# Attention into a gated MLP on one core: PSUM score banks lent to four steps of the second h phase, and small VectorE work moved around it

## The chip, the cores and the metric

The kernel runs on one core of one Trainium2 chip. The metric is the device time of one execution in microseconds; for each kernel the median of several runs is taken. One further execution is taken with the hardware profiler, and all durations of single instructions come from that one.

## The reference, cut to what matters

Eight batches, eight heads, 512 local tokens and 32 global tokens of width 64. Local queries see the global keys and a window of 32 keys on either side; global queries see all keys. The 544 tokens of each batch then go through an MLP with a gate of the quick-gelu form.

```python
s_g = scale * q_g @ concat(k_g, k_l).T         # global queries: all keys
out_g = softmax(s_g) @ concat(v_g, v_l)
s_ll = where(abs(i - j) <= 32, scale * q_l @ k_l.T, -1e9)
s_lg = scale * q_l @ k_g.T                     # local queries: global keys + window
out_l = softmax(concat(s_lg, s_ll)) @ concat(v_g, v_l)
x = concat(out_g, out_l) as (tokens, heads * 64)         # 512 features
h = x @ w_in                                   # 512 -> 2048
out = (h * sigmoid(1.702 * h)) @ w_out         # 2048 -> 512
```

Inputs and outputs are float32; the products run on bf16 operands with float32 sums.

## The kernel before, in words

**Units of work.** A batch's eight heads are two groups of four; a group is one object, `a` (heads 0 to 3) and `c` (heads 4 to 7) of the batch in hand. Batches 0 and 1 use the class `Quad`, batches 2 to 7 the class `Wide`. The objects of batch 2 are `nq[2]`.

**What an object does.** `Tk` turns k (VectorE stream transpose of a 128x512 tile, line 525, and a copy of a part of it, line 527), `Tq` turns q (line 308), `ext` places the group's global queries around the turned q and the global keys into the turned k (four small VectorE copies, lines 536 to 540, from `qgT` and `kgT`, which `transpose_g` fills, line 238). `S(0)` and `S(1)` are the two rounds of scores: TensorE writes them into a *pair* (`spair`): two PSUM tiles of two banks each, named s0 and s1. `X` is the exponential, one ScalarE instruction for each of the two tiles (line 562), `M` the multiplication with the mask on VectorE (line 567). `U(0)` to `U(2)` sum weights and values on TensorE, `Gm` does so for global queries, and `R`, `XL` and `G` divide and store the result as the MLP's input (`xL`, `xG`) on VectorE. For batch 2 onward `UG` is `U` and `Gm`, `RXG` the divisions.

**The MLP.** For a batch i, `h_step(i, fc)` runs one of 16 steps: four matmuls of 512 columns into one PSUM bank (`h_mm`, line 606), tanh of it on ScalarE into `th` (line 613), and on VectorE the product of 1 + tanh and the bank (line 614), which is the gate's output `gT`. `th` has two buffers. The banks come from `pbank`, a pool of four one-bank tiles, which also serves the sums of `U`, `Gm` and the output. `phase_o(i)` then multiplies with `w_out` in four blocks of 16 matmuls (`o`, line 631), and each block is evicted on ScalarE (line 645) and stored.

**Order.** The program is written out by hand: `manual_schedule` keeps each engine's queue in the order in which the Python code issues instructions. Each engine runs its queue in order; semaphores between the engines are placed by the framework, from which instruction touches which tile. The attention of batch i + 1 stands between the h phase and the four o blocks of batch i: at the end of an h phase, `a.S(0)` of the next batch has been done; `phase_o` begins with `c.T()`, `c.ext()`, `a.S(1)`, `a.X(1)`, `a.M(1)`, `o(0)`, `c.S(0)`, `a.UG()`.

**The second h phase** (i = 1) is written out apart from the others, since it still has work of batch 2 in it. Its four first half-steps and the extra work per step read:

```python
for fc, kcs in ((0, (0, 1)), (1, (0, 1)), (0, (2, 3)), (1, (2, 3))):
    h_mm(1, fc, hps[fc], kcs)
for fc in range(FC):
    h_act(1, fc, hps[fc]) if fc < 2 else h_step(1, fc)
    if fc == 1: nq[1][1].G()
    if fc == 2: a.Tk()
    if fc == 7: transpose_g(4, 6, "q"); a.ext()
    if fc == 10: a.S(0); a.X(0)
a.M(0)
```

Just before it, the same pair of score tiles holds sums of batch 1: `a.Gm` in bank 0 and the three sums of `c` in banks 1 to 3; `c.XL` and `a.G` read them last. `nq[2][0].Tq()` and `transpose_g(4, 6, "k")` stand behind `a.R()` of batch 1.

## Time and profile before

| | |
|---|---|
| median of 3 runs | 303.69 us (303.2 to 304.45) |
| the profiled execution, as timed | 303.15 us |
| its span, first to last instruction | 301.4 us |
| TensorE busy | 292.7 us, 97% |
| VectorE busy | 218.3 us, 72% |
| ScalarE busy | 167.3 us, 56% |
| GpSimd busy | 75.5 us, 25% |
| share of the chain that ended last | TensorE 84%, VectorE 5%, DMA 4%, ScalarE 4% |
| mean granted TensorE clock | 1.000 |

In the profile's lines PE is TensorE, PEld its weight loads, DVE VectorE, ACT ScalarE, POOL GpSimd and SP the queue that issues output DMAs. A line of a timeline gives start (us from the start of the span), duration (us; of a merged group, first start to last end), engine, source line, operation, tiles and shape, count, and in brackets the engine's idle time before it and what ended it. In the list of groups by form, the two numbers behind the bar are the total in us and the mean of one in ns. Matmuls overlap: each shows some 0.38 us of 512 columns, and one starts every 0.216 us.

The stage at issue, by the trace's windows: from 54.07 to 69.74 us (second h phase) TensorE is busy 15.14 of 15.67 us, VectorE 12.91 and ScalarE 10.77; from 90.50 to 104.31 us (third h phase) TensorE is busy 13.81 of 13.81 us, VectorE 10.20 and ScalarE 9.55.

### The profile page before, as it was taken

Reading aid. Unit: us, or ns where it says so; the run is one execution under the profiler, and the core shown is the slowest. Engines: PE = TensorE matmul, PEld = TensorE weight load, DVE = VectorE, ACT = ScalarE, POOL = GpSimd, SP = SyncE. Lnnn points to the kernel's source line nnn. Section 1 sums busy time; section 2 is a strip of 40 time slices with the busy share of each in tenths; the row PEclk is TensorE's granted clock in tenths of the full one; section 3 lists DMA queues with packets and bytes.
Section 4 is the critical chain, followed back from the end, with each engine's and each line's share of the span. In section 5 each row is a group of like instructions: output and inputs, shape, how many; then the busy total and the mean of one; then the engine's idle time right before and its main releaser. Section 6 shows DMA issues by size and latency. Waiting matters only on the chain.

```text
span 301.4 us, 8146 instructions
## 1 busy us (share of the span) xinstructions
PE 292.7 (97%) x3409; PEld 150.1 (50%) x3409; DVE 218.3 (72%) x445; ACT 167.3 (56%) x258; POOL 75.5 (25%) x126
## 2 busy tenths in 40 slices
PE   6899999998999999999999999999999999999995
PEld 6454445443554455445454455445454455446653
DVE  6578857879976887778967887788877866683320
ACT  4838484476537756476446736567447651763421
POOL 8742655972045000900054002600000000000000
PEclk9999999999999999999999999999999999999999
DMA  7999999999459512990269412900220012101122
GB/s 191 178 209 209 206 180 226 123 181 183 66 78 145 100 37 54 124 153 7 70 70 145 86 38 72 124 0 11 63 63 10 0 48 64 35 0 28 44 69 71
DMA packets 59220, 28.35 MB, mean 94 GB/s; under 512 B 47664, under 2 KB 49072, under 8 KB 59184
## 3 DMA queue, kind: packets, MB, share of 16 engines
q0 software_dynamic: 51024, 17.57, 51.9%
q1 hardware_dynamic: 7680, 9.61, 12.0%
q10 hardware_dynamic: 480, 0.66, 0.7%
q8 instruction: 26, 0.43, 0.6%
q14 instruction: 10, 0.08, 0.1%
HBM read 36.31 MB, written 8.91 MB: 150 GB/s over the span
## 4 chain that ended last, share of the span: by engine, by line
PE 84%; DVE 5%; DMA 4%; ACT 4%; issue 1%; SPq 0%; ACTq 0%
PE op L631 35%; PE hp L606 33%; PE ov L577 5%; PE s L551 4%; DVE gT L614 2%; DMA ek<-ek 2%; DMA g32k<-in_k_g_dram 2%; ACT th L613 1%; PE s L606 1%; ACT e L380 1%; PE ov L459 1%; PE op L643 1%; ACT e L562 1%; DVE e L567 1%; DVE kT L525 1%
## 5 line engine op out<-in xcount | busy, mean ns | idle before, releaser
L631 PE MATMUL op<-w_out_sb,gT 128*128 128x512 bf16 x528 | 121.8, 380 | 0.0
L614 DVE SCALAR_TENSOR_TENSOR gT<-th,hp 128x512 bf16<-128x512 f32 (+1 forms) x140 | 91.2, 657 | 41.3 <-ACT th L613 40.2
L606 PE MATMUL hp<-xL,w_in_sb 128*128 128x512 bf16 x496 | 109.2, 379 | 0.5 <-DVE xL L492 0.2
L613 ACT ACTIVATE th<-hp 128x512 f32<-128x512 f32 (+1 forms) x140 | 79.8, 573 | 43.9 <-PE hp L606 39.7
L606 PEld LDWEIGHTS <-w_in_sb 128*128 128x128 bf16 x576 | 56.1, 98 | 65.4 <-issue 1.8
L631 PEld LDWEIGHTS <-gT 128*128 128x128 bf16 x528 | 49.3, 98 | 55.3 <-issue 0.9
L645 ACT ACTIVATE ob<-op 128x512 f32<-128x512 f32 (+2 forms) x35 | 20.5, 585 | 71.8 <-PE op L631 69.3
L97 POOL DMA_DIRECT2D v<-in_v_l_dram x30 | 23.9, 800 | 98.3 <-PE og L588 94.0
L562 ACT ACTIVATE e<-s 128x1016 bf16<-128x1016 f32 (+1 forms) x48 | 45.7, 1005 | 1.2 <-PE s L551 1.0
L567 DVE TENSOR_TENSOR e<-e,mask 128x1760 bf16<-128x1760 bf16 (+1 forms) x24 | 25.0, 1040 | 2.2 <-ACT e L562 2.2
L483 DVE STREAM_TRANSPOSE sT<-ov 128x512 f32<-128x512 f32 x15 | 10.8, 717 | 15.5 <-PE ov L577 11.6
L492 DVE TENSOR_TENSOR xL<-ov,rs 128x512 bf16<-128x512 f32 x30 | 19.3, 686 | 1.5 <-PE ov L459 0.2
L551 PE MATMUL s<-q,kT 32*128 32x160 bf16 (+3 forms) x576 | 16.1, 243 | 0.9 <-DVE kT L540 0.9
L551 PEld LDWEIGHTS <-kT 32*128 32x128 bf16 x576 | 11.1, 94 | 11.3 <-issue 5.1
L380 ACT ACTIVATE e<-s 128x856 bf16<-128x856 f32 x14 | 11.7, 881 | 5.1 <-PE s L347 5.1
L99 POOL DMA_DIRECT2D v<-in_v_g_dram x24 | 13.9, 580 | 2.4 <-DMA rk<-in_k_l_dram 2.1
L525 DVE STREAM_TRANSPOSE kT<-rk 128x512 f32<-128x512 f32 x12 | 12.5, 1041 | 0.0
L487 DVE STREAM_TRANSPOSE rs<-rT 128x512 f32<-128x512 f32 x16 | 11.4, 711 | 0.6
L308 DVE STREAM_TRANSPOSE q<-rq 128x512 f32<-128x512 f32 (+1 forms) x17 | 11.3, 662 | 0.2 <-ACT rq L669 0.2
L577 PE MATMUL ov<-e,v 128*32 128x128 bf16 (+3 forms) x576 | 11.0, 223 | 0.0
L606 PE MATMUL hp<-xG,w_in_sb 128*128 128x256 bf16 x64 | 9.6, 273 | 0.0
L577 PEld LDWEIGHTS <-v 128*32 128x32 bf16 x576 | 9.1, 97 | 0.1
(105 smaller groups left out, 173.8 us busy)
## 6 DMA issues: line engine op xcount, KB each, us to landing
out_dram<-ob SPq DMA_DIRECT2D x132, 64.0 KB, 1.9
rk<-in_k_l_dram POOLq DMA_DIRECT2D x6, 512.0 KB, 9.4
rq<-in_q_l_dram POOLq DMA_DIRECT2D x5, 512.0 KB, 7.5
v<-in_v_l_dram POOLq DMA_DIRECT2D x24, 96.0 KB, 4.5
w_out_sb<-in_moe_w_out_dram POOLq DMA_DIRECT2D x4, 512.0 KB, 10.5
v<-in_v_l_dram POOLq DMA_DIRECT2D x14, 128.0 KB, 6.7
rq<-in_q_l_dram POOLq DMA_DIRECT2D x5, 256.0 KB, 8.9
w_in_sb<-in_moe_w_in_dram POOLq DMA_DIRECT2D x4, 256.0 KB, 6.7
```

The lines of the kernel that those rows point to most:

```text
L97: nc.gpsimd.dma_start(out=vt[0:n, :, c, :D], in_=vs[FIRST[c] : FIRST[c] + n])
L492: nc.vector.tensor_mul(self.x[:, 2 * self.u + h, :], self.st[1 + h], self.st["rs"])
L525: nc.vector.transpose(flat[:, 0:Sl].rearrange("p (r t) -> p t r", t=16), loaded[self.b][0][:, self.u].bitcast(F32))
L551: nc.tensor.matmul(bank(self.ps, j)[:, at : at + n], lhsT=self.k[p, KEYS[c] : KEYS[c] + 128, e], rhs=self.q[p, lo:hi, r0 : r0 + nr, e], st ...
L562: nc.scalar.activation(self.E[rnd][:, 2 * i : 2 * i + 2, :n], self.ps[i][:, :, :n], AF.Exp, scale=scale)
L567: nc.vector.tensor_mul(e, e, mask[:, rnd : rnd + 1, :n].to_broadcast([128, 4, n]))
L577: nc.tensor.matmul(ov[32 * j : 32 * j + 32, :].rearrange("p (t r) -> p t r", t=16)[:, t0:t1, r0 : r0 + nr], lhsT=lv, rhs=self.E[rnd][:, j, ...
L606: nc.tensor.matmul(hp[:, : width(i)], lhsT=w_in_c[:, fc // 8, kc, fc % 8 // 2, :, fc % 2], rhs=(xL[i] if i < B else xG)[:, kc, :], start=( ...
L613: nc.scalar.activation(th[:, :n], hp[:, :n], AF.Tanh, scale=0.851)
L614: nc.vector.scalar_tensor_tensor(gTs[i][:, fc, :n], in0=th[:, :n], scalar=1.0, in1=hp[:, :n], op0=ALU.add, op1=ALU.mult)
L631: nc.tensor.matmul(op, lhsT=gTs[i][:, fc, tci * 128 : tci * 128 + 128], rhs=w_out_sb[:, fc, :], start=(first and fc == 4 * f4), stop=(fc = ...
L645: nc.scalar.activation(ob[:, lo:hi], op[:, lo:hi], AF.Copy, scale=0.5)
```

## The change

Five edits, all but the last in or just before the second h phase:

1. `nq[2][0].Tq()` and the transpose of batch 2's global k move from behind `a.R()` to behind `c.M(0)` of batch 1.
2. `a.Tk()` of batch 2 moves from behind step 2 to the front of the phase, the transpose of global q from step 7 to step 1, and `nq[1][1].G()` from step 1 to step 2.
3. Steps 2 to 5 take the four banks of a new pair of score tiles (banks 2, 3, 0, 1, so steps 2 and 3 share tile s1, steps 4 and 5 tile s0) in place of banks of the pool.
4. The four copies of `a.ext()` go to ScalarE, one behind the tanh of each of steps 3 to 6, and three of the four of `c.ext()` behind those of steps 7 to 9; the fourth stays on VectorE. The two exponentials of `a.X(0)` stand behind the tanh of step 10 and of step 11.
5. `ext` addresses the same bytes as two-byte elements, twice as many, in all phases, so also where its copies stay on VectorE.

```diff
-        def ext(self):
+        def ext(self, parts=range(4), copy=None):
+            copy = copy or nc.vector.tensor_copy
+            qt = self.qt.bitcast(BF16)
+            qg = qgT[:, self.Q, :].bitcast(BF16)
             def g(n, r, m):
-                src = qgT[:, self.Q, : n * r].rearrange("p (t o r) -> p t o r", o=1, r=r)
-                return src.to_broadcast([128, n, m, r])
-            ends = self.qt[:, 0:4, :].rearrange("p t (g r) -> p t g r", r=8)
-            nc.vector.tensor_copy(ends[:, :, 0:4:3], g(4, 8, 2))
-            nc.vector.tensor_copy(self.qt[:, 20:23, 4:28].rearrange(...), g(3, 12, 2))
-            nc.vector.tensor_copy(self.qt[:, 1:4, 10:22], qgT[:, self.Q, :36].rearrange(...))
-            nc.vector.tensor_copy(self.kT[:, :, 96:128], kgT[:, self.Q : self.Q + 1].to_broadcast([128, 4, 32]))
+                src = qg[:, : 2 * n * r].rearrange("p (t o r) -> p t o r", o=1, r=2 * r)
+                return src.to_broadcast([128, n, m, 2 * r])
+            if 0 in parts:
+                copy(qt[:, 0:4, :].rearrange(...)[:, :, 0:4:3], g(4, 8, 2))
+            if 1 in parts:
+                copy(qt[:, 20:23, 8:56].rearrange(...), g(3, 12, 2))
+            if 2 in parts:
+                copy(qt[:, 1:4, 20:44], qg[:, :72].rearrange(...))
+            if 3 in parts:
+                copy(self.kT.bitcast(BF16)[:, :, 192:256],
+                     kgT[:, self.Q : self.Q + 1].bitcast(BF16).to_broadcast([128, 4, 64]))
...
-        def X(self, rnd):
+        def X(self, rnd, halves=(0, 1)):
...
     c.M(0)
+    nq[2][0].Tq()
+    transpose_g(4, 6, "k")
     osteps(0, (2, 2), (2, 3))
...
     a.R()
-    nq[2][0].Tq()
-    transpose_g(4, 6, "k")
     c.M(1)
...
+    a.Tk()
     gTs[1] = moe.tile([128, FC, TB], BF16, name="gT")
     hps = [pbank("hp") for _ in range(2)]
     for fc, kcs in ((0, (0, 1)), (1, (0, 1)), (0, (2, 3)), (1, (2, 3))):
         h_mm(1, fc, hps[fc], kcs)
+    pt = spair()
+    hps += [bank(pt, j) for j in (2, 3, 0, 1)]
+    def on_act(out_, in_):
+        nc.scalar.activation(out_, in_, AF.Copy)
     for fc in range(FC):
         if fc < 2:
             h_act(1, fc, hps[fc])
         else:
-            h_step(1, fc)
+            h_step(1, fc, hps[fc] if fc < 6 else None)
         if fc == 1:
+            transpose_g(4, 6, "q")
+        if fc == 2:
             nq[1][1].G()
-        if fc == 2:
-            a.Tk()
-        if fc == 7:
-            transpose_g(4, 6, "q")
-            a.ext()
+        if 3 <= fc <= 6:
+            a.ext((fc - 3,), on_act)
+        if 7 <= fc <= 9:
+            c.ext((fc - 7,), on_act)
         if fc == 10:
             a.S(0)
-            a.X(0)
+            a.X(0, (0,))
+        if fc == 11:
+            a.X(0, (1,))
     a.M(0)
...
         c.T()
-        c.ext()
+        c.ext((3,) if i == 1 else range(4))
```

More of the change, by code (lines that the diff above doesn't have):

```diff
@@ L528, in Tk @@
             self.k = flat.bitcast(BF16).rearrange("p (m e) -> p m e", e=2)
-        def ext(self):
+        def ext(self, parts=range(4), copy=None):
+            copy = copy or nc.vector.tensor_copy
+            qt = self.qt.bitcast(BF16)
+            qg = qgT[:, self.Q, :].bitcast(BF16)
             def g(n, r, m):
-                src = qgT[:, self.Q, : n * r].rearrange("p (t o r) -> p t o r", o=1, r=r)
-                return src.to_broadcast([128, n, m, r])
-            ends = self.qt[:, 0:4, :].rearrange("p t (g r) -> p t g r", r=8)
-            nc.vector.tensor_copy(ends[:, :, 0:4:3], g(4, 8, 2))
-            nc.vector.tensor_copy(self.qt[:, 20:23, 4:28].rearrange("p t (g r) -> p t g r", r=12), g(3, 12, 2))
-            nc.vector.tensor_copy(self.qt[:, 1:4, 10:22],
-                                  qgT[:, self.Q, :36].rearrange("p (t r) -> p t r", r=12))
-            nc.vector.tensor_copy(self.kT[:, :, 96:128], kgT[:, self.Q : self.Q + 1].to_broadcast([128, 4, 32]))
+                src = qg[:, : 2 * n * r].rearrange("p (t o r) -> p t o r", o=1, r=2 * r)
+                return src.to_broadcast([128, n, m, 2 * r])
+            if 0 in parts:
+                copy(qt[:, 0:4, :].rearrange("p t (g r) -> p t g r", r=16)[:, :, 0:4:3], g(4, 8, 2))
+            if 1 in parts:
+                copy(qt[:, 20:23, 8:56].rearrange("p t (g r) -> p t g r", r=24), g(3, 12, 2))
+            if 2 in parts:
+                copy(qt[:, 1:4, 20:44], qg[:, :72].rearrange("p (t r) -> p t r", r=24))
+            if 3 in parts:
+                copy(self.kT.bitcast(BF16)[:, :, 192:256],
+                     kgT[:, self.Q : self.Q + 1].bitcast(BF16).to_broadcast([128, 4, 64]))
         def S(self, rnd):
@@ L557, in S @@
             self.E[rnd] = att.tile([128, 4, EW], BF16, name="e%d" % rnd)
-        def X(self, rnd):
+        def X(self, rnd, halves=(0, 1)):
             n = (EW, EW - 12)[rnd]
-            for i in range(2):
+            for i in halves:
                 nc.scalar.activation(self.E[rnd][:, 2 * i : 2 * i + 2, :n], self.ps[i][:, :, :n], AF.Exp, scale=scale)
@@ L615, in h_act, with h_step @@
                                        in1=hp[:, :n], op0=ALU.add, op1=ALU.mult)
-    def h_step(i, fc):
+    def h_step(i, fc, hp=None):
         if fc == 0:
             gTs[i] = moe.tile([128, FC, TB], BF16, name="gT")
-        hp = pbank("hp")
+        if hp is None:
+            hp = pbank("hp")
         h_mm(i, fc, hp, range(NKC))
```

## The prediction, made before the changed kernel was run

> **What bounds the kernel now.** First the page's table of engines, for what is short.

> ```profile
> PE 292.7 (97%) x3409; PEld 150.1 (50%) x3409; DVE 218.3 (72%) x445; ACT 167.3 (56%) x258; POOL 75.5 (25%) x126
> ```

> TensorE hardly rests, so a change can save only its gaps. The granted clock is 1.000, so the clock plays no part. Second, the chain of waits in order of time (start us, us, engine and line), for where a gap lies:

> ```profile
> 52.23 1.85 PE op L631 x8
> 54.07 1.29 DVE xL L492 x2
> 55.40 0.39 PE hp L606
> 55.82 0.61 ACT th L613
> 56.45 1.28 DVE gT L614 x2
> ...
> 61.60 0.70 DVE gT L614
> 62.38 0.61 ACT th L613
> 63.01 0.69 DVE gT L614
> ...
> 70.87 0.69 DVE gT L614
> 71.56 0.98 DVE e L567
> ...
> 74.89 0.68 PE s L551 x24
> 75.57 1.51 PE ov L577 x70
> ...
> 90.50 13.81 PE hp L606 x64
> ```

> Later h phases are one piece of TensorE: 64 matmuls, 13.81 us, 0.216 each, 0.863 a step. Between start-up and the last batch, the second h phase (54.07 to 74.89) is the one stage where the chain runs through VectorE and ScalarE. A th buffer pair makes the loop: tanh k waits for product k-2, and two steps take 63.01 - 61.60 = 1.41 us. Third, TensorE's timeline there:

> ```profile
> 69.74 0.66 PE L551 MATMUL s<-q,kT 32*128 32x108 bf16 x24
> 74.89 0.68 PE L551 MATMUL s<-q,kT 32*128 32x160 bf16 x24 [0.92 <-DVE kT L540]
> ```

> From 54.07 to 69.74 are 15.67 us for 13.81 of h and 0.61 of scores: 1.25 lost. Then scores 0.60 and o 3.56 end at 73.90 and the next scores start at 74.89: 0.99 lost. The sums after them take 1.51 where later phases show 1.20: 0.31 lost. So 2.55 us is all that this place can give. Fourth, VectorE's timeline before and in it:

> ```profile
> 47.72 0.72 DVE L483 STREAM_TRANSPOSE sT<-ov 128x512 f32<-128x512 f32 x1 [1.31 <-PE ov L459]
> 49.40 0.67 DVE L308 STREAM_TRANSPOSE q<-rq 128x512 f32<-128x512 f32 x1
> 49.99 0.20 DVE L238 STREAM_TRANSPOSE kgT<-rkg 128x64 f32<-128x64 f32 x1
> ...
> 58.90 1.04 DVE L525 STREAM_TRANSPOSE kT<-rk 128x512 f32<-128x512 f32 x1
> 59.98 0.30 DVE L527 COPY kT<-kT 128x192 f32<-128x192 f32 x1
> ```

> **A walk through the phase.** I go step by step with these rows: matmul 0.216 apart, a step's sum ready 0.17 after its last slot (a matmul shows 0.38); tanh 0.60, starting 0.03 after the sum and 0.08 after product k-2; product 0.69, 0.03 after its tanh, the next one 0.60 later if nothing holds it; TensorE resumes 0.05 after a VectorE end (55.35 to 55.40). For the kernel before it gives an end of h at 69.76 (trace 69.74), of product 15 at 71.48 (71.56) and of the second mask (M(1), line 567) at 75.71 (75.79). I compare walk with walk.

> **Transposes of q and global k moved up.** They leave 49.40 to 50.12 and stand after c.M(0), which ends at 46.41; VectorE then idles 1.31 us until 47.72, and they take about 0.85. Their loads were issued at 32.70 and 33.22; the slowest such load took 10.1 and 13.8 us, so they land by 47.0 at the worst. VectorE is full from 47.72 to 55.35, so all behind moves 0.73 up: the c.XL pair ends at 54.62, and the 0.22 that TensorE waits for it goes.

> **a.Tk() moved up.** 1.30 us (58.90 to 60.20), now behind a.G() (0.68) and ahead of product 0. Its load (issued 40.50, at most 9.6) lands by 50.1. Queued behind it are all products: product 0 starts at 54.54 (the pair's successor, 1.21 after 53.33) + 0.68 + 1.30 = 56.52, not 56.45, product 1 at 57.12. tanh 2 needs product 0, so 57.21 + 0.08 = 57.29; product 2 is 57.92 to 58.61. Global q's transpose (0.2) fits between; c.G() moves behind product 2.

> **Score banks for steps 2 to 5.** With more banks TensorE would not wait for early products; I expect it to wait longer. A pair of score banks is two tiles of two banks each; steps 2 and 3 share one, steps 4 and 5 the other, and each step's product is issued before the next step's matmuls. The instruction order of the changed program lists these waits (the first matmul of steps 2, 3 and 5; the first one waits on TensorE's own count):

> ```
> L613 Matmult s4_1223<-xL_758,w_in_sb_114 128x512 [waits PE_49]
> L613 Matmult s4_1223<-xL_758,w_in_sb_114 128x512 [waits DVE_49]
> L613 Matmult s4_1222<-xL_758,w_in_sb_114 128x512 [waits DVE_49]
> ```

> The counts asked for are those of product 2 and product 4: step 3 may not write its own bank until the reader of the neighbour bank is done. TensorE is in order, so all h behind it waits. Walk: step 2 is done at 56.66, step 3 resumes after 58.61, counted from 58.83: 2.17 lost. It ends at 59.69, step 4 at 60.55; tanh 4 60.58, product 4 61.21 to 61.90; step 5 from 62.12: 1.57 lost. The ten steps from there run free, with the scores, to 62.98 + 8.63 + 0.61 = 72.22. So 3.74 is added and the 1.25 removed; steps 6 and on wait for nothing, since VectorE has caught up. [...]

> **Copies on ScalarE.** Seven of 72 to 256 two-byte elements. Nearest rows: a 32-element eviction, 0.20, and the 128x160 and 128x192 mask copies, 0.49 and 0.55, which gives 0.35 to 0.65 each on their slope. In the first h phase a tanh and such a copy took 0.87 to 0.92 a step, TensorE's pace. They fall in steps 3 to 9, where ScalarE now waits on TensorE: nothing on the path at either price (last product 73.57 both ways). Without the two waits, the dear end would cost 0.4. Splitting the exponentials moves one tanh 0.9 sooner and the next later: nothing, as X is read only by M(0).

> **The end of the stage.** Product 15 ends 1.35 after h: 73.57 (71.48). Then VectorE's queue: M(0), c.T, one copy in place of four (0.28 saved), M(1). From product 15 to the end of M(1) were 4.23, now 3.95: 77.52 against 75.71. The scores start at 73.57 + 3.03 (2.78 from 71.56 to the copies at 74.34, the copy 0.2, the wake-up 0.05) = 76.60, TensorE being ready at 72.22 + 0.60 + 3.56 = 76.38: of the 0.99 remains 0.22. Behind that, TensorE has no wait until the last batch, so the shift stays: **+1.81 us**.

> **Two-byte view in the other phases.** The four VectorE copies now count twice the elements. At 107.46 to 107.87 they take 0.41; M(1) ends at 108.91, needed about 109.2. If they doubled, some 0.1 would be lost in each of five phases: 0 to 0.5, nothing gained as the slack is unused. No row of the trace is such a copy; I take 0, since the nearest rows (166 to 216 ns for 36 to 128 wide elements) are mostly a fixed part. [...] POOL's and SP's orders are unchanged.

> **Sum.** 303.15 (the profiled execution: span 301.4 and 1.75 around) + 1.81 = 304.96. The median of the runs, 303.69, is 0.54 above that run; on it I forecast **305.5 us**.

> **Rivals.** *Faster: the two waits don't bite.* Without them the walk ends h at 68.49, product 15 at 69.84, M(1) at 73.79: -1.92, 301.8 us. It decides when both waits together cost under 1.9 us. For it: nothing in the trace shows such a wait. Against: the order lists it, and product 2 cannot be early with Tk ahead. 0.06. *Only the first wait bites* (product 4 early): 3.74 - 1.57, the stage ends 0.25 late, 303.9 us. For it: ScalarE is idle there. Against: step 4's own sum, tanh and product take 1.35 after it. 0.13. *The transposes find no gap*, the XL pair stays at 55.35: both waits move with it, +2.5, 306.2 us. Against: the landings. 0.13. *The two-byte copies cost*: +2.3, 306.0 us. 0.08. The forecast keeps 0.60.

> **Numbers.** 0.5% (1.5 us) is about what a measurement can tell from no change. The forecast is 0.3 above that bound; with a spread of half a us from row times and run medians I count 0.42 of its 0.60 as slower, 0.18 as same. Slower 0.42 + 0.13 + 0.08 = 0.63; same 0.18 + 0.13 = 0.31; faster 0.06. The range 304.2 to 306.6 leaves out the faster rival and most of the one-wait case.

> **What would show it.** Right: TensorE idle about 2.0 and 1.4 us before steps 3 and 5, released by the gT product, no other gap in h; scores after o about 1.7 late; VectorE's XL pair ending near 54.6. Wrong: one h piece without gaps from 54 on (rival one), ScalarE copies over 0.65, or later scores waiting on kT's copy by more than 0.1.

## The result, and the profile after

Over 22 runs of each, the changed kernel has a median of 307.02 us (304.9 to 311.67) and the kernel before 303.74 us: ratio 1.0096, interval 1.0073 to 1.0118 (executions over 1.5% above the fastest of their kernel are left out of the ratio). It is slower, as forecast, but by 3.3 us where 1.8 were forecast, and the time lies above the range (304.2 to 306.6).

One thing is needed to read this number. In 12 of the 22 executions the mean granted TensorE clock is 0.999 or 1.000, with a median of 305.85 us. In the other ten it is 0.982 to 0.994, and these take 307.69 to 311.67 us. For the kernel before, the clock is on record for the 64 executions that were run beside the experiments below: 55 of them are at 0.997 or above, with a median of 303.77 us. So the change costs 305.85 - 303.77 = 2.08 us where the clock stays full, and the rest of the 3.3 us comes from a clock that does not.

The profiled execution of the changed kernel has a full clock: 305.89 us, span 304.0 (before 303.15 and 301.4). First, its page's table of engines:

```profile
PE 291.1 (96%) x3368; PEld 151.2 (50%) x3409; DVE 217.8 (72%) x438; ACT 168.6 (55%) x265; POOL 75.6 (25%) x126
```

TensorE's share has sunk by a point: the span grew, the work did not. (The matmul count differs from 3409 only by records that the trace lacks.) Second, TensorE's timeline in the changed stage:

```profile
54.56 1.89 PE L613 MATMUL hp<-xL,w_in_sb 128*128 128x512 bf16 x8
56.28 1.03 PE L613 MATMUL s<-xL,w_in_sb 128*128 128x512 bf16 x4
59.34 1.89 PE L613 MATMUL s<-xL,w_in_sb 128*128 128x512 bf16 x8 [2.03 <-DVE gT L621]
62.70 1.02 PE L613 MATMUL s<-xL,w_in_sb 128*128 128x512 bf16 x4 [1.47 <-DVE gT L621]
63.56 4.48 PE L613 MATMUL hp<-xL,w_in_sb 128*128 128x512 bf16 x19
...
77.45 0.68 PE L558 MATMUL s<-q,kT 32*128 32x160 bf16 x24 [0.22 <-DVE kT L546]
```

`s` is the lent score tile. TensorE idles 2.03 us before step 3 and 1.47 us before step 5, both times until a product (gT) has ended; no other gap is left in h. In the trace of the kernel before, h starts with

```profile
53.90 1.29 PE L606 MATMUL hp<-xL,w_in_sb 128*128 128x512 bf16 x5
```

so that from the first h matmul to the batch 1 scores after o the stage takes 77.45 - 54.56 = 22.89 us, against 74.89 - 53.90 = 20.99 before: +1.90. The span grew by 2.6; the other 0.7 is there ahead of the stage (h starts at 54.56 where 53.90 is before's, though nothing before 46 us was changed): ScalarE's casts in the start-up wait 2.6 us for loads of q, 0.9 in the trace of before. Two more full-clock traces of the same kernel start h at 54.26 and 54.81. Third, the chain of waits there:

```profile
57.28 1.19 DVE gT L621 x2
58.48 0.15 DVE qgT L238
58.63 0.67 DVE gT L621
...
59.34 1.90 PE s L613 x8
...
61.33 0.61 ACT th L620
...
61.96 0.70 DVE gT L621
...
62.70 1.02 PE s L613 x4
```

It goes product 0, 1, the transpose of global q, product 2, then step 3's matmuls, step 4's, its tanh, its product, step 5's matmuls: the chain of the prediction's walk. Fourth, VectorE's timeline ahead of the stage:

```profile
47.08 0.70 DVE L308 STREAM_TRANSPOSE q<-rq 128x512 f32<-128x512 f32 x1
47.71 0.20 DVE L238 STREAM_TRANSPOSE kgT<-rkg 128x64 f32<-128x64 f32 x1
...
54.02 1.29 DVE L492 TENSOR_TENSOR xL<-s,rs 128x512 bf16<-128x512 f32 x2
```

The two transposes found the gap behind the mask at line 387, and the XL pair ends at 55.31, 0.75 after h started.

### The profile page after: what moved, and what is told of

It reads as the page before. It is cut to its first block, busy times and chain, and to the rows that moved or that the text cites. A ratio compares the mean times of both kernels' runs of the same rounds, so it can differ in the third digit from the quotient of the medians.

```text
span 304.0 us, 8105 instructions
## 1 busy us (share of the span) xinstructions
PE 291.1 (96%) x3368; PEld 151.2 (50%) x3409; DVE 217.8 (72%) x438; ACT 168.6 (55%) x265; POOL 75.6 (25%) x126
## 4 chain that ended last, share of the span: by engine, by line
PE 84%; DVE 6%; DMA 4%; ACT 3%; issue 2%; SPq 0%; ACTq 0%; DVEq 0%
PE hp L613 35%; PE op L639 33%; PE ov L584 5%; PE s L558 5%; DMA ek<-ek 2%; PE s L613 2%; DMA q<-in_q_l_dram 2%; DVE gT L621 2%; ACT e L380 1%; PE ov L459 1%; DVE xL L492 1%; PE s L347 1%; PE ov L433 1%; PE op L651 1%; DVE e L574 1%
## 5 line engine op out<-in xcount | busy, mean ns | idle before, releaser
L639 PE MATMUL op<-w_out_sb,gT 128*128 128x512 bf16 x497 | 119.1, 379 | 1.9 <-issue 0.5
L621 DVE SCALAR_TENSOR_TENSOR gT<-th,hp 128x512 bf16<-128x512 f32 (+1 forms) x136 | 88.7, 655 | 41.4 <-ACT th L620 40.7
L613 PE MATMUL hp<-xL,w_in_sb 128*128 128x512 bf16 x472 | 104.8, 379 | 0.4
L620 ACT ACTIVATE th<-hp 128x512 f32<-128x512 f32 (+1 forms) x136 | 77.4, 572 | 40.3 <-PE hp L613 38.7
L613 PEld LDWEIGHTS <-w_in_sb 128*128 128x128 bf16 x576 | 56.1, 98 | 68.0 <-issue 4.1
L483 DVE STREAM_TRANSPOSE sT<-ov 128x512 f32<-128x512 f32 x15 | 10.8, 717 | 14.4 <-PE ov L584 11.5
L492 DVE TENSOR_TENSOR xL<-ov,rs 128x512 bf16<-128x512 f32 x30 | 19.3, 685 | 1.4
L525 DVE STREAM_TRANSPOSE kT<-rk 128x512 f32<-128x512 f32 x12 | 12.5, 1040 | 0.0
L308 DVE STREAM_TRANSPOSE q<-rq 128x512 f32<-128x512 f32 (+1 forms) x17 | 11.3, 664 | 1.5 <-ACT rq L677 1.5
L613 PE MATMUL s<-xL,w_in_sb 128*128 128x512 bf16 x31 | 7.3, 379 | 3.7 <-DVE gT L621 3.5
L613 PE MATMUL hp<-xG,w_in_sb 128*128 128x256 bf16 x64 | 9.6, 273 | 0.0
```

Of the source, the lines that this page charges most:

```text
L492: nc.vector.tensor_mul(self.x[:, 2 * self.u + h, :], self.st[1 + h], self.st["rs"])
L613: nc.tensor.matmul(hp[:, : width(i)], lhsT=w_in_c[:, fc // 8, kc, fc % 8 // 2, :, fc % 2], rhs=(xL[i] if i < B else xG)[:, kc, :], start=( ...
L620: nc.scalar.activation(th[:, :n], hp[:, :n], AF.Tanh, scale=0.851)
L621: nc.vector.scalar_tensor_tensor(gTs[i][:, fc, :n], in0=th[:, :n], scalar=1.0, in1=hp[:, :n], op0=ALU.add, op1=ALU.mult)
L639: nc.tensor.matmul(op, lhsT=gTs[i][:, fc, tci * 128 : tci * 128 + 128], rhs=w_out_sb[:, fc, :], start=(first and fc == 4 * f4), stop=(fc = ...
```

## The experiments

The theory: the lent banks make two waits, because what a matmul waits for is kept by tile and not by bank, and those two waits also let the granted clock fall to half in some of the executions. The rivals: the longer runs are mere variation between launches (rival N); the waits come from the banks themselves and not from the shared tile (rival B); the copies on ScalarE or the transposes cost something too. Stage lengths below run, as above, from the first h matmul to the batch 1 scores after o. Every ratio is to runs of the kernel before in the same series; series lie on different chips.

**The changed kernel again.**

> The changed kernel again, beside the others. Theory W+C (two waits on the neighbour bank cost 1.8 us, and the idle that they make lets the TensorE clock drop in some executions): runs in two groups, near 305.8 us with mean clock 1.0 and near 308.4 with mean clock about 0.988, some half of each. Rival N (the spread is noise of the host or of the loads at the start, the same for every kernel): the kernel before shows the same share of long runs on the same chip.

Measured 307.29 us (6 runs), ratio 1.0108 (1.0072 to 1.0144). Three runs have clocks of 0.987 to 0.994 and 308.02 to 308.75 us; the other three have a median of 306.03. The two groups are there again; of the 23 runs of the kernel before in this series, one has a clock below 0.997.

**Same schedule, gaps filled with matmuls that nobody reads.**

```diff
+    hps.append(pbank("hp"))
...
+            if fc in (3, 5):
+                keep(8 if fc == 3 else 6, hps[6])
-            h_step(1, fc, hps[fc] if fc < 6 else None)
+            h_step(1, fc, hps[fc] if fc < 7 else None)
```

> The changed kernel with 8 and 6 matmuls on zeros put on TensorE ahead of steps 3 and 5, into a free bank: 1.73 and 1.30 us of work inside the two waits of about 2.0 and 1.5 us, so the schedule stays that of the changed kernel. Theory W+C: the stage ends as late as in the changed kernel (+1.8 us), all runs near 305.6 us with mean clock 1.0, no group near 308.4. Rival N: two groups as in the changed kernel.

TensorE's timeline of this kernel (line 174 is the filler):

```profile
56.95 1.89 PE L174 MATMUL hp<-warm 128*128 128x512 bf16 x8
59.08 1.89 PE L613 MATMUL s<-xL,w_in_sb 128*128 128x512 bf16 x8 [0.24 <-DVE gT L621]
60.81 1.46 PE L174 MATMUL hp<-warm 128*128 128x512 bf16 x6
62.44 1.02 PE L613 MATMUL s<-xL,w_in_sb 128*128 128x512 bf16 x4 [0.17 <-DVE gT L621]
```

Steps 3 and 5 start where they did (4.72 and 8.08 us after h; 4.78 and 8.14 in the changed kernel), and the stage has 22.84 us. Measured 305.41 us (305.17 to 306.11), ratio 1.0056 (1.0037 to 1.0074), and none of 6 runs below a clock of 0.997. More work for TensorE, the same waits, and 1.9 us less in the median than the changed kernel beside it: what goes with the filler is the idle time, so rival N has little left (though six runs each are few).

**The first wait made longer:** `a.Tk()`'s transpose and copy done two more times.

```diff
     a.Tk()
+    for _ in range(2):
+        nc.vector.transpose(a.kT.rearrange("p c s -> p (c s)")[:, 0:Sl].rearrange("p (r t) -> p t r", t=16),
+                           loaded[2][0][:, 0].bitcast(F32))
+        nc.vector.tensor_copy(a.kT[:, 2:4, 0:96], a.kT[:, 0:2, 96:192])
```

> The changed kernel with the work of a.Tk (transpose and copy, 1.3 us) done three times ahead of product 0: the first wait grows by about 2.6 us, to 4.6; values unchanged. Theory W+C: the stage ends 4.4 us later than in the kernel before, and the TensorE clock falls to half for some 7 us in nearly every run, near 311 us with mean clock about 0.988; the profile's clock row shows where. Rival N: 308 us, clock 1.0.

Measured 310.74 us (309.95 to 314.84), ratio 1.0216 (1.0186 to 1.0247); all 5 runs at clocks from 0.977 to 0.993. Its trace shows where the clock falls. The table by stretches; the columns are the stretch, its us, busy us of TensorE, its weight loads, VectorE, ScalarE and GpSimd (instructions in brackets), granted clock, DMA share, GB/s:

```profile
60.00:63.00 3.00, 0.70 (x4) 0.20 (x2) 2.86 (x5) 0.53 (x2) 3.00 (x5) 1.00 0.91 173
63.00:66.00 3.00, 0.46 (x2) 0.18 (x2) 2.89 (x9) 0.60 (x1) 1.75 (x3) 0.52 1.11 223
66.00:69.00 3.00, 3.00 (x8) 0.95 (x7) 0.85 (x2) 0.80 (x2) 1.78 (x3) 0.50 2.20 163
69.00:72.00 3.00, 1.53 (x5) 0.54 (x4) 0.69 (x1) 0.81 (x2) 2.74 (x4) 0.50 1.87 174
72.00:76.00 4.00, 4.00 (x17) 1.62 (x15) 2.01 (x3) 2.74 (x7) 0.00 (x0) 0.83 1.15 202
```

and TensorE's timeline of the same trace:

```profile
65.54 3.57 PE L613 MATMUL s<-xL,w_in_sb 128*128 128x512 bf16 x8 [4.84 <-DVE gT L621]
70.58 1.87 PE L613 MATMUL s<-xL,w_in_sb 128*128 128x512 bf16 x4 [1.47 <-DVE gT L621]
```

The clock halves inside the first wait, and eight matmuls that took 1.89 us take 3.57, four that took 1.02 take 1.87. By the clocks of these stretches (0.52 over 3 us is 2.88 us at half rate, 0.83 over 4 us is 1.36) this lasts 2.88 + 3.00 + 3.00 + 1.36 = 10.24 us, three times 3.41. The stage has 28.75 us, 7.8 more than before where 4.4 were expected: the 4.4 left out the half rate, and the two groups of matmuls above make up 2.5 of the other 3.4.

**Where the drop lies in the changed kernel itself:** two more traces of it.

> The changed kernel once more, for one trace: about half of its executions show a mean clock near 0.988. If the half clock belongs to the two waits of the stage, a trace with such a mean shows the windows of half clock after the wait before step 3 (59 to 69 us) and the time near 308.5 us; a trace with a mean of 1.000 shows 306 us. If it belongs to the start-up, whose loads vary, the windows lie before 20 us and the stage has its 22.9 us in either case.

> As the trace before it: the same kernel a second time, since a trace shows the drop in about one of two executions.

308.29 us at a clock of 0.994, and 305.55 us at 0.999. The first contradicts the simple form of the theory. Its table by stretches, same columns, and its TensorE timeline:

```profile
9.00:12.00 3.00, 2.72 (x46) 1.51 (x46) 2.67 (x11) 2.26 (x4) 2.02 (x3) 0.64 2.34 153
12.00:15.00 3.00, 3.00 (x60) 1.50 (x57) 0.23 (x1) 2.33 (x5) 3.00 (x6) 0.79 1.51 195
```

```profile
61.27 1.89 PE L613 MATMUL s<-xL,w_in_sb 128*128 128x512 bf16 x8 [2.03 <-DVE gT L621]
64.62 1.02 PE L613 MATMUL s<-xL,w_in_sb 128*128 128x512 bf16 x4 [1.47 <-DVE gT L621]
```

The half clock is one stretch of some 3.4 us in the start-up, where TensorE waits for loads, and the stage runs at full clock with its usual two waits. In the other trace the waits were 2.25 and 1.47 us and no clock fell anywhere (1.00 in every stretch of its tables). So a mean of 0.994 (half clock for 3.4 of 304 us: 1 - 0.5 x 3.41/304) can be the start-up's, and the kernel before has four executions at 0.993 or 0.994 too. What sets the changed kernel apart are the longer drops, 0.991 and below: 11 of its 30 executions in all, against 2 of 64 of the kernel before and 3 of 67 of all the versions here without two unfilled waits of that size in a row (the filled one among them). A single short drop in the stage would read 0.994 as well, so this count can miss some. Their median among the 22 runs is 309.06 us, 3.2 above the full-clock ones; two windows at half rate lose at most 3.41. That these drops sit in the two waits is an inference from these counts, from the trace with the longer wait and from the next experiment's: no trace caught one in the changed kernel.

**Edit 3 alone, on the kernel before.**

```diff
...
+    pt = spair()
+    hps += [bank(pt, j) for j in (2, 3, 0, 1)]
...
-            h_step(1, fc)
+            h_step(1, fc, hps[fc] if fc < 6 else None)
```

> The kernel before with the lent banks alone, every other edit left out. Theory W: waits of about 2.0 and 1.4 us for the products of steps 2 and 4, the stage ends 2.75 us later than in the kernel before (by the walk 78.46 against 75.71), clean runs at 306.4 us; theory C: about half of the runs some 2.6 us longer with mean clock near 0.988. Rival M (the banks only cost together with the early Tk): within 0.5 us of the kernel before.

Measured 306.53 us (305.67 to 311.73, 6 runs), ratio 1.008 (1.0048 to 1.0111). The five full-clock runs have 306.5, 2.8 above those of the kernel before in this series (303.70): the lent banks are the loss, and the other edits give back some 0.7 of it. That half of its runs would be long was wrong: one of six. Its profile is that run; it has one window of half clock in the start-up (0.50 from 12 to 14 us) and one behind the first wait (0.54 from 63 to 66 us):

```profile
63.08 3.47 PE L606 MATMUL s<-xL,w_in_sb 128*128 128x512 bf16 x8 [1.96 <-DVE gT L614]
68.01 1.02 PE L606 MATMUL s<-xL,w_in_sb 128*128 128x512 bf16 x4 [1.47 <-DVE gT L614]
```

Eight matmuls in 3.47 us: here half clock followed a wait of 1.96 us.

**Banks of the pool again, all other edits kept.**

```diff
-    pt = spair()
-    hps += [bank(pt, j) for j in (2, 3, 0, 1)]
...
-            h_step(1, fc, hps[fc] if fc < 6 else None)
+            h_step(1, fc)
```

> Steps 2 to 5 take banks of the pool as in the kernel before; the other edits stay. By the walk step 3 waits 0.8 us for product 0 (late behind Tk), the stage ends at 74.56 against 75.71: 1.15 us faster than the kernel before, about 302.5 us (ratio 0.996), clock 1.0. Rival M: at or above 305 us.

Measured 302.58 us (302.15 to 304.27, 12 runs), ratio 0.9961 (0.9943 to 0.9978), no run below 0.997; the stage has 19.81 us, 1.18 less than before. The edits without the lent banks make the kernel faster.

**Bank or tile: the four lent banks in another order,** so that neighbouring steps lie in different tiles.

```diff
-    hps += [bank(pt, j) for j in (2, 3, 0, 1)]
+    hps += [bank(pt, j) for j in (2, 0, 3, 1)]
```

> The changed kernel with the banks of the pair in the order 2, 0, 3, 1: neighbouring steps lie in different tiles, and step 4 waits for product 2, step 5 for product 3. Theory W (the wait is for the reader of the same tile): idle of 1.3 us before step 4 and 0.4 before step 5, none before step 3, the stage ends 0.2 us sooner than in the kernel before, 303.5 us, clock 1.0 in most runs. Rival B (any lent bank makes its step wait): as the changed kernel, 305.8 us and two groups.

```profile
59.60 1.02 PE L613 MATMUL s<-xL,w_in_sb 128*128 128x512 bf16 x4 [1.18 <-DVE gT L621]
60.85 1.02 PE L613 MATMUL s<-xL,w_in_sb 128*128 128x512 bf16 x4 [0.23 <-DVE gT L621]
```

In its TensorE timeline step 3 waits for nothing; steps 4 and 5, which now share tiles with steps 2 and 3, wait 1.18 and 0.23 us. Same four banks, so the wait belongs to the tile and rival B falls. 303.88 us (12 runs), ratio 1.0003 (0.9979 to 1.0028); stage 20.79.

**All matmuls of steps 2 to 5 ahead of the products.**

```diff
+    for fc in range(2, 6):
+        h_mm(1, fc, hps[fc], range(NKC))
...
-        if fc < 2:
+        if fc < 6:
             h_act(1, fc, hps[fc])
         else:
-            h_step(1, fc, hps[fc] if fc < 6 else None)
+            h_step(1, fc)
```

> Steps 2 to 5: all their matmuls are issued ahead of the first product, so that no matmul follows the reader of its neighbour bank; all else as in the changed kernel. Theory W+C: no wait of TensorE inside the h phase, the second mask of the stage ends 1.9 us sooner than in the kernel before (73.8 against 75.7 by the walk), median about 301.8 us (ratio 0.994), mean clock 1.0 in all runs. Rival M (the moved Tk, the ScalarE copies or the two-byte copies cost the time): still above 305 us.

Measured 302.71 us (12 runs), ratio 0.9965 (0.9946 to 0.9984); one run has a clock of 0.989, where 1.0 was expected in all. The two waits are gone, but the stage is 1.28 shorter than before, not the 1.92 expected. ScalarE's timeline says why:

```profile
57.45 0.60 ACT L620 ACTIVATE th<-s 128x512 f32<-128x512 f32 x1 [1.07 <-PE s L613]
58.80 0.60 ACT L620 ACTIVATE th<-s 128x512 f32<-128x512 f32 x1 [0.76 <-DVE gT L621]
```

The tile rule holds for readers too: tanh 2 starts only when step 3's matmuls into the neighbour bank are done, and tanh 3, whose sum has long been ready, only when VectorE has read the neighbour bank (58.80).

**Lent banks for steps 2 and 3 alone.**

```diff
-    hps += [bank(pt, j) for j in (2, 3, 0, 1)]
+    hps += [bank(pt, j) for j in (2, 3)]
...
-            h_step(1, fc, hps[fc] if fc < 6 else None)
+            h_step(1, fc, hps[fc] if fc < 4 else None)
```

> The changed kernel with only steps 2 and 3 in lent banks (one pair tile), steps 4 and 5 in banks of the pool: the first wait stays, the second goes. Theory W: idle of 2.0 us before step 3 alone, the stage ends 0.25 us later than in the kernel before, 303.9 us. Theory C: one idle stretch of 2 us drops the clock in fewer runs than two within 6 us (under a third, against half). Rival N: half of the runs long, as in the changed kernel.

One wait, of 2.34 us, is left. 304.26 us (12 runs), ratio 1.0019 (0.9995 to 1.0042); the stage is 0.58 longer than before where 0.25 was expected. No clock was at 0.991 or below in 12 runs, and one was at 0.994, so one such wait by itself does not do it often.

**Pool banks, the extension copies on VectorE where they were.**

```diff
-        if 3 <= fc <= 6:
-            a.ext((fc - 3,), on_act)
-        if 7 <= fc <= 9:
-            c.ext((fc - 7,), on_act)
+        if fc == 7:
+            a.ext()
...
-        c.ext((3,) if i == 1 else range(4))
+        c.ext()
```

> Pool banks for steps 2 to 5 and the small copies of batch 2 on VectorE again (two-byte view), the rest as changed. By the walk the copies fit into VectorE's slack inside h and cost only at the end of the stage: 0.28 us later than with pool banks and ScalarE copies. Rival M (the ScalarE copies bring most of the gain): over 0.7 later.

One trace of each: the stage has 20.09 us, 0.28 more than with the copies on ScalarE. Edit 4 is worth what the prediction gave it.

**Pool banks, and `a.Tk()` behind step 4.** To the kernel with pool banks:

```diff
-    a.Tk()
...
+        if fc == 4:
+            a.Tk()
```

> Pool banks for steps 2 to 5, and a.Tk behind step 4 in place of ahead of product 0; the other edits stay. By the walk the stage ends at 74.11, 0.45 sooner than with pool banks and an early Tk, 1.6 sooner than the kernel before: about 302.1 us (ratio 0.9947). Rival M (the early Tk costs nothing): as with pool banks alone, ratio 0.996.

The shortest stage: 19.35 us, 1.64 less than before and 0.46 less than with the early `a.Tk()`, where 0.45 was expected. Measured 302.15 us (301.33 to 305.7, 12 runs), ratio 0.9963 (0.9933 to 0.9994), full-clock median 302.06. The times do not tell it from the pool banks with an early `a.Tk()` (0.9961); that the early one costs something rests on one trace of each. In its TensorE timeline h is one piece up to the first scores, 44 matmuls in 9.93 us without a gap.

## Why the prediction was right and wrong

**The step that failed** is the sentence "The granted clock is 1.000, so the clock plays no part." It was read from one execution of the kernel before, which has no such waits, and taken over to a kernel into which the same text puts 3.74 us of TensorE idling within six. The sum has no term for it. The runs put one there: in 11 of 30 executions long drops, some 3.2 us each. With one short drop, of a kind that the kernel before has as well, ten of the 22 timed executions were below full clock, and the median moved from 305.85 to 307.02. Full-clock executions alone would have lain in the range, 0.35 above the forecast.

The traces show a granted clock of 0.50 in such a drop (66 to 72 us with the longer wait), lengths in multiples of 3.41 us (10.24 there), and windows that lie elsewhere in each execution (last section). They give no one length of wait that decides: half clock followed a wait of 1.96 us in one trace (edit 3 alone), and did not follow one of 2.25 in another (the changed kernel at 305.55 us).

**The stage was right in place and size.** Forecast: idle about 2.0 and 1.4 us before steps 3 and 5, released by the product; measured 2.03 and 1.47. Forecast: scores at 76.60, counted from an h start of 53.90, thus 22.70 us; measured 22.89, so +1.90 against +1.71. The end of the wait for kT, 0.22, is the trace's 0.22, and the XL pair's end, 0.72 after h began in the walk, is 0.75.

**ScalarE copies** took 0.25 to 0.41 us, most of them less than the bound of 0.35 to 0.65. Two of the seven, in ScalarE's timeline,

```profile
60.90 0.30 ACT L833 ACTIVATE q<-qgT 128x128 bf16<-128x128 bf16 x1
65.18 0.41 ACT L833 ACTIVATE kT<-kgT 128x256 bf16<-128x256 bf16 x1
```

stand there with nothing on the path, as taken. The mask copies were the wrong neighbours: one of 160 elements took 0.49 us, a copy of 144 here takes 0.31. Why is not shown.

**The two-byte view** cost nothing, also as taken: the copy of kT, 128 elements of four bytes before and 256 of two after, is 216 ns in both traces, and from the batch 1 scores after o to the end of the span are 226.5 us before and 226.6 after. No run shows the 0.5 us that the rival with costly two-byte copies counts with; in its place the medians of the four VectorE copies are 165, 199, 174 and 216 ns before and 165, 198, 174 and 216 ns after.

**The rivals.** "The waits don't bite" falls; its price was off too, -1.92 where the two versions without them gave -1.28 and -1.18. With lent banks the tile rule holds tanh back; with pool banks the early `a.Tk()` holds the products back, and moving that gives -1.64. "Only the first wait bites" falls; the kernel built like it gave +0.58, not +0.25. The transposes found their gap, and the copies cost nothing.

## What to carry to other kernels

Borrowing a bank of a tile that spans two banks borrowed the whole tile's waits here: matmuls into one bank waited for the reader of the other (2.03 and 1.47 us before steps 3 and 5), and tanh of one bank for the other's writer and reader (1.07 and 0.76 us with all matmuls ahead). So neighbouring steps belong in different tiles (ratio 1.0003 where the changed kernel has 1.0096) or in a pool (0.9961). When a change puts idle time into a TensorE that hardly rested (97% busy before), add a clock term to the sum and time many executions: one profile shows one draw, and long drops came in 11 of 30 here. If such a wait can't be avoided, matmuls that nobody reads may fill it; here they took the median from 307.29 to 305.41 us in the same series of runs.

## What the hardware showed that was not expected

The granted clock fell to half for stretches of 3.41 us and its multiples (10.24 us in one trace) with far less idle than a whole stretch ahead of it: after 1.96 us in the stage once, and in the start-up of another trace after waits of 0.37 and 1.22 us for loads. With waits of 2.03 and 1.47 us some 3.4 apart, long drops came in 11 of 30 executions; with 4.84 and 1.47 in 4 of 5; with a single 2.34 in none of 12; with the gaps filled in none of 6. With edit 3 alone, waits of 1.96 and 1.47, it was 1 of 6.
